# Second FFN of a fused attention and two-FFN kernel: each tile's last product moved one tile later, tile 1 turned by TensorE, other order of copies and joins

## Chip, cores, metric

The kernel runs on one core of a Trainium2 chip. The metric is the device time of one execution in microseconds (us); smaller is better. Engines are named as in the profile: PE (TensorE matmul), PEld (TensorE weight load), DVE (VectorE), ACT (ScalarE), POOL (GpSimd), SP (the queue that issues the DMAs).

## What is computed

Block attention over q, k, v of shape (2, 8, 768, 64), a first FFN with 2048 hidden columns, and a second FFN with 1024 hidden columns, all over 1536 tokens of width 512. The change touches the second FFN alone:

```python
def _moe2_ref(x, w_in, w_out, g_ln):          # x: 1536 x 512
    h = x @ w_in                              # 1536 x 1024
    h_max = np.max(h, axis=-1, keepdims=True)
    e = np.exp(h - h_max)
    sm = e / (np.sum(e, axis=-1, keepdims=True) + 1e-09)
    solu = h * sm
    mu = np.mean(solu, axis=-1, keepdims=True)
    var = np.mean((solu - mu) ** 2, axis=-1, keepdims=True)
    ln = (solu - mu) / np.sqrt(var + 1e-06) * g_ln
    return (ln @ w_out).astype(np.float32)    # 1536 x 512
```

## The kernel before, in words

The order of the program is written out by hand; every engine works through its own instructions strictly in that order, and semaphores make it wait for others. Each float32 factor of a product is split into a high and a low part, and a product is three passes (high x high, high x low, low x high).

The 1536 tokens are 12 tiles of 128 rows (t = 0 to 11), taken two at a time as pairs (p = 0 to 5; tiles 2p and 2p+1). For the first product a pair's input is combined into sums and split: `sum_xo` (4 subtractions or additions on POOL, L862) and `split_xo` (four pieces 0 to 3; a high part, on POOL a cast at L886 or on ACT at L884, and a low part on POOL, L887). With them seven products of six matmuls each, `emit_m(p, ...)` (L899, 42 in all), give both tiles' h: first products 1, 6, 7 and 5, each in a PSUM bank of its own (0, 1, 2 and 3), then 2, 4 and 3 in banks 0, 1 and 2 again. Before these three can write, the first four must be read: `emit_p1` copies bank 0 on ACT (L907), `emit_u2` and `emit_u3` read banks 1 and 2 on DVE (L911, L918), `emit_t5` bank 3 (L921). `emit_block` adds and takes the row maxima in PSUM (DVE, L930 to L936). The even tile ends in banks 1 and 3, the odd one in banks 0 and 2.

Then a tile t goes through these steps:

- `emit_exp2(t)`: exp on ACT from PSUM into e (L946), two halves; `emit_mult2(t)`: h times e on DVE (L952), which frees the tile's two banks.
- `emit_stats(t)` and `emit_factors(t)`: mean and variance on DVE (L961 to L974), and at the end a power on POOL, `pow` (L975).
- `emit_scaled(t)`: DVE takes the result of pow (L979) and scales e (L980).
- e must be turned for the last product, its columns on the partitions. By DMA: `emit_planes(t)` separates the two 16-bit halves on ACT (L1023, two instructions) and SP issues two DMA transposes (L1026); `emit_join(t, halves)` puts them together again, for each half of the tile a gather on ACT (L1036), the high part on ACT (L1039) and the low part on POOL (L1040), into the tile's place `ls`. By TensorE: `turn(t, banks)` makes 8 transposes into two banks (L1007), the high part on ACT (L1008), the low part on DVE (L1009). Before, tiles 0, 10 and 11 are turned by TensorE and the others by DMA.
- `emit_o2(t, bank)`: the last product, 24 matmuls (L1063), and `emit_out(t)`: a copy of the bank on ACT (L1073) and the output DMA.

PSUM has eight banks of this kind: four serve the even pairs, four the odd ones (`pair_banks`). `emit_o2` writes into banks of the pair before the current one, after `emit_mult2` has freed them, and the pair after next can use them once `emit_out` has copied them. The turned tiles have four places (`ls_places`, t % 4). The buffers "s" (three of 128 x 512) are shared in turn by `sum_xo` and `emit_join`; "raw" (three) by planes and turned planes.

In the loop before (L1207), step p holds: products of pair p, the join of tile 2p-2, last products of tiles 2p-3 and 2p-2, exp and statistics of the pair, the join of tile 2p-1, planes of tile 2p, sums and splits of pair p+2. Step 1 differs: pair 1's products come ahead of the loop, and its planes and join of tile 1 stand in the loop's tail:

```python
            if p == 1:
                emit_out(0)
                emit_planes(1)
            ...
            if p < NPT - 1:
                emit_planes(f)
            if p == 1:
                emit_join(1)
```

## Time and profile before

| | us |
|---|---|
| median of 3 runs | 499.28 (499.1 to 502.49) |
| the profiled execution's own time | 499.53 |
| its span, first to last instruction | 497.6 |
| busy in the span: PE, PEld | 471.0, 387.5 |
| busy in the span: DVE, ACT, POOL | 314.8, 319.5, 219.5 |

The profiled execution lasted 1.93 us longer than its span. A span is read from the first to the last instruction of any engine; a row of the timeline gives its start, its length, engine, line, operation, the tiles it writes and reads, and in brackets how long the engine stood idle ahead of it and what ended that. Rows that follow each other closely on one engine and line are merged, with a count. Matmuls are pipelined, so the distance between starts tells more than their lengths. The granted clock is given as a share of the full 2.4 GHz.

### The profile page before, as it was taken

Reading aid. Unit: us, or ns where it says so; the run is one execution under the profiler, and the core shown is the slowest. Engines: PE = TensorE matmul, PEld = TensorE weight load, DVE = VectorE, ACT = ScalarE, POOL = GpSimd, SP = SyncE. Lnnn points to the kernel's source line nnn. Section 1 sums busy time; section 2 is a strip of 40 time slices with the busy share of each in tenths; the row PEclk is TensorE's granted clock in tenths of the full one; section 3 lists DMA queues with packets and bytes.
Section 4 is the critical chain, followed back from the end, with each engine's and each line's share of the span. In section 5 each row is a group of like instructions: output and inputs, shape, how many; then the busy total and the mean of one; then the engine's idle time right before and its main releaser. Section 6 shows DMA issues by size and latency. Waiting matters only on the chain.

```text
span 497.6 us, 8050 instructions
## 1 busy us (share of the span) xinstructions
PE 471.0 (95%) x2907; PEld 387.5 (78%) x2907; DVE 314.8 (63%) x752; ACT 319.5 (64%) x566; POOL 219.5 (44%) x220
## 2 busy tenths in 40 slices
PE   8999899999999999999999999999997099999997
PEld 4878777778888888888888888888886088888886
DVE  3978775664444554746566465747999386877840
ACT  2688788757576756656655565657724677878721
POOL 2688788424323222222327237352054678683310
PEclk9999999999999999999999999999999589999999
DMA  7899974001332232232222121202102214133111
GB/s 214 243 237 236 227 197 137 5 1 43 106 106 86 88 122 88 84 112 100 86 96 74 42 85 44 85 1 84 43 1 63 63 23 126 42 87 105 42 43 43
DMA packets 59047, 46.18 MB, mean 93 GB/s; under 512 B 40448, under 2 KB 51328, under 8 KB 59008
## 3 DMA queue, kind: packets, MB, share of 16 engines
q1 hardware_dynamic: 59008, 45.67, 31.8%
q8 instruction: 23, 0.38, 0.3%
q14 instruction: 16, 0.13, 0.1%
HBM read 36.61 MB, written 3.15 MB: 80 GB/s over the span
## 4 chain that ended last, share of the span: by engine, by line
PE 77%; DVE 8%; ACT 4%; DMA 3%; POOL 3%; issue 2%; SPq 2%; POOLq 0%; ACTq 0%
PE y L319 25%; PE h L277 25%; PE h L1063 12%; PE h L899 9%; PE sps L562 2%; DMA vt<-in_v_dram 2%; PE vsum L473 1%; DMA qt<-in_q_dram 1%; DVE e L952 1%; PE aps L599 1%; SPq L445 1%; DVE e L980 1%; POOL sm L577 1%; POOL w L187 1%; ACT at L604 1%
## 5 line engine op out<-in xcount | busy, mean ns | idle before, releaser
L277 PE MATMUL h<-xs,w 128*128 128x512 f32 x576 | 141.2, 391 | 0.0
L319 PE MATMUL y<-gs,w 128*128 128x512 f32 x576 | 138.2, 389 | 0.0
L319 PEld LDWEIGHTS y<-gs,w 128*128 128x128 f32 x576 | 108.0, 188 | 22.5
L277 PEld LDWEIGHTS h<-xs,w 128*128 128x128 f32 x576 | 107.2, 188 | 21.6
L187 POOL TENSOR_TENSOR w<-s,w 128x512 fp32r<-128x512 f32 x32 | 41.7, 1303 | 102.8 <-ACT w L186 95.3
L286 ACT ACTIVATE r<-h 128x512 int32<-128x512 f32 x48 | 28.6, 597 | 87.1 <-PE h L277 87.0
L291 DVE SCALAR_TENSOR_TENSOR r<-r,h 128x512 f32<-128x512 int32 x48 | 33.0, 687 | 71.0 <-ACT r L286 70.8
L899 PE MATMUL h<-w,xo 128*128 128x512 f32 x252 | 60.9, 400 | 14.4 <-ACT p L907 14.4
L899 PEld LDWEIGHTS h<-w,xo 128*128 128x128 f32 x252 | 48.8, 194 | 25.1 <-ACT p L907 14.8
L1063 PE MATMUL h<-w,ls 128*128 128x512 f32 (+1 forms) x312 | 66.9, 373 | 0.0
L169 DVE SCALAR_TENSOR_TENSOR s<-raw 128x512 int32<-128x512 int32 x48 | 37.6, 783 | 44.6 <-ACT raw L163 43.4
L1063 PEld LDWEIGHTS h<-w,ls 128*128 128x128 f32 x312 | 55.3, 188 | 10.3
L296 ACT ACTIVATE r<-r,half_pi 128x512 f32<-128x512 f32 x48 | 34.6, 721 | 5.4 <-DVE r L291 5.3
L301 DVE TENSOR_TENSOR h<-h,r 128x512 f32<-128x512 f32 x48 | 33.0, 688 | 4.9 <-ACT r L296 4.8
L307 DVE TENSOR_TENSOR gs<-h,gs 128x512 fp32r<-128x512 f32 x48 | 32.7, 680 | 5.3 <-ACT gs L306 5.3
L1040 POOL TENSOR_TENSOR ls<-s,ls 128x512 fp32r<-128x512 f32 x18 | 23.3, 1293 | 20.4 <-ACT ls L1039 20.4
L162 ACT ACTIVATE raw<-raw 128x512 f32<-128x512 f32 x48 | 31.9, 664 | 0.2 <-DMA raw<-in_moe_w_in_dram 0.2
L163 ACT ACTIVATE raw<-raw 128x512 int32<-128x512 uint32 x48 | 32.0, 666 | 0.0
L770 POOL TENSOR_TENSOR w<-s,w 128x512 fp32r<-128x512 f32 x14 | 17.9, 1293 | 30.8 <-ACT w L769 30.8
L306 ACT ACTIVATE gs<-h 128x512 fp32r<-128x512 f32 x48 | 28.2, 587 | 0.4 <-DVE h L301 0.4
L577 POOL TENSOR_TENSOR sm<-sm,mx 128x480 f32<-128x480 f32 x24 | 24.6, 1025 | 8.0 <-DVE mx L573 8.0
L592 POOL TENSOR_TENSOR sm<-sm,ss 128x480 f32<-128x480 f32 x24 | 26.2, 1094 | 0.3 <-ACT at L604 0.2
(103 smaller groups left out, 666.1 us busy)
## 6 DMA issues: line engine op xcount, KB each, us to landing
raw<-in_moe_w_in_dram SPq DMA_DIRECT2D x24, 512.0 KB, 3.6
raw<-in_moe_w_out_dram SPq DMA_DIRECT2D x24, 512.0 KB, 3.6
vt<-in_v_dram SPq DMA_DIRECT2D x16, 240.0 KB, 5.3
kt<-in_k_dram SPq DMA_DIRECT2D x8, 384.0 KB, 5.1
qt<-in_q_dram SPq DMA_DIRECT2D x8, 384.0 KB, 6.8
out_dram<-osb SPq DMA_DIRECT2D x11, 256.0 KB, 2.0
vt<-vm SPq DMA_DIRECT2D x16, 72.0 KB
vt<-in_v_dram SPq DMA_DIRECT2D x16, 48.0 KB, 6.8
```

Source lines behind the costliest of these rows:

```text
L162: nc.scalar.activation(out=hw, in_=hw, func=AF.Prelu, scale=REBIAS, alpha=NEGATIVE)
L163: nc.scalar.activation(out=lw, in_=lw.bitcast(U32), func=AF.Copy, scale=TOP3)
L169: nc.vector.scalar_tensor_tensor(out=self.f32[i], in0=t[:, :, 1], scalar=3, in1=t[:, :, 0], op0=ALU.logical_shift_left, op1=ALU.bitwise_or)
L187: nc.gpsimd.tensor_tensor(out=w[:, 1, :], in0=f, in1=as32(w[:, 0, :]), op=ALU.subtract)
L277: nc.tensor.matmul(h, lhsT=w[:, a, f * P:(f + 1) * P], rhs=xs_of[tb, c][:, b_, :], start=(m == 0), stop=(m == 3 * KC - 1))
L291: nc.vector.scalar_tensor_tensor(out=r, in0=r.bitcast(I32), scalar=TWO_PI, in1=h_of[step], op0=ALU.mult, op1=ALU.subtract)
L296: nc.scalar.activation(out=r, in_=r, func=AF.Sin, scale=-1.0, bias=half_pi)
L301: nc.vector.tensor_tensor(out=h, in0=h, in1=r, op=ALU.mult)
L307: nc.vector.tensor_tensor(out=gs[:, 1, :], in0=r, in1=as32(gs[:, 0, :]), op=ALU.subtract)
L319: nc.tensor.matmul(y[e], lhsT=w[:, a, e * P:(e + 1) * P], rhs=gs[:, b_, :], start=(f == 0 and i == 0), stop=(f == GF - 1 and i == 2))
L899: nc.tensor.matmul(banks_of[p][BANK[m]], lhsT=x[:, a, s0:s0 + P], rhs=w2_of[m, c][:, b_, :], start=c == j == 0, stop=c == 1 and j == 2)
L1063: nc.tensor.matmul(o, lhsT=ls_of[t][f // 4][:, a, s0:s0 + P], rhs=w[:, b_, cols], start=(f == 0 and i == 0), stop=(f == NF2 - 1 and i == 2))
```

## The change

The loop over pairs begins at 3 in place of 1; steps 1 and 2 are written out ahead of it. Throughout, the last product of a tile comes one tile later than it did: in step p those of tiles 2p-4 and 2p-3 (before: 2p-3 and 2p-2), so that three tiles are left behind the loop in place of two. The even and odd tiles' results go to other banks (1 and 3 of the pair before, in place of 0 and 1). Tile 1 is turned by TensorE, not by DMA. `emit_join` can make the high part on POOL (L1042 after, a cast), and does so for tiles 5 to 9. The copy `emit_p1(2)` stands ahead of any planes; sums and splits of a pair stand elsewhere among the joins and pows. No product is left out or added but the 8 transposes of tile 1.

```diff
-        def emit_join(t, halves=(0, 1)):
+        def emit_join(t, halves=(0, 1), hi=nc.scalar):
...
-                nc.scalar.activation(out=l[:, 0, :], in_=as32(s), func=AF.Copy)
+                if hi is nc.scalar:
+                    nc.scalar.activation(out=l[:, 0, :], in_=as32(s), func=AF.Copy)
+                else:
+                    hi.tensor_copy(l[:, 0, :], as32(s))
...
-        for p in range(1, NPT):
...
+        def emit_xo(p):
+            sum_xo(p)
+            split_xo(p, (0, 1, 2, 3), nc.gpsimd)
+
+        def complete(p, *products):
+            for m in products:
+                emit_m(p, m)
+                emit_block(p, m)
...
+        O = banks_of[0]
+        emit_o2(0, O[3])
+        emit_exp2(2)
+        emit_exp2(3)
+        emit_mult2(2)
+        emit_stats(2)
+        sum_xo(3)
+        emit_factors(2)
+        emit_out(0)
+        banks_of[2] = pair_banks(2)
+        emit_m(2, 1, 6, 7, 5)
+        emit_p1(2)
+        emit_u2(2)
+        emit_mult2(3)
+        emit_u3(2)
+        turn(1, banks_of[1][1::2])
+        emit_scaled(2)
+        emit_planes(2)
+        split_xo(3, (0, 1), nc.gpsimd)
+        emit_stats(3)
+        emit_factors(3)
+        emit_t5(2)
+        emit_block(2, 5)
+        emit_scaled(3)
+        emit_planes(3)
+        split_xo(3, (2, 3), nc.gpsimd)
+        complete(2, 2, 4, 3)
+        emit_o2(1, banks_of[1][2])
+        sum_xo(4)
+        split_xo(4, (0, 1), nc.gpsimd)
...
+        emit_out(1)
+        banks_of[3] = pair_banks(3)
+        emit_m(3, 1, 6, 7, 5)
+        emit_p1(3)
+        emit_join(2, (0,))
+        split_xo(4, (2, 3), nc.gpsimd)
+        emit_exp2(4)
+        emit_exp2(5)
+        emit_join(2, (1,))
+        emit_u2(3)
+        emit_u3(3)
+        emit_mult2(4)
+        emit_t5(3)
+        emit_block(3, 5)
+        emit_stats(4)
+        emit_factors(4)
+        emit_mult2(5)
+        emit_scaled(4)
+        complete(3, 2, 4, 3)
+
+        for p in range(3, NPT):
             f, s = 2 * p, 2 * p + 1
             O = banks_of[p - 1]
...
+            hi = nc.gpsimd if p > 3 else nc.scalar
+            emit_o2(f - 4, O[1])
+            emit_join(f - 3, (0, 1), hi)
+            emit_o2(f - 3, O[3])
+            if p == 3:
+                emit_planes(4)
+                emit_xo(5)
             emit_exp2(f)
             emit_exp2(s)
+            emit_out(f - 4)
+            emit_stats(s - 2)
+            emit_factors(s - 2)
             emit_mult2(f)
...
+            emit_scaled(s - 2)
+            if p < NPT - 1:
+                emit_planes(s - 2)
+                emit_stats(f)
                 emit_out(f - 3)
...
+                banks_of[p + 1] = pair_banks(p + 1)
+                emit_m(p + 1, 1, 6, 7, 5)
+                emit_factors(f)
+                emit_p1(p + 1)
+                emit_join(f - 2, (0, 1), hi)
+                emit_mult2(s)
+                emit_u2(p + 1)
+                emit_scaled(f)
                 emit_planes(f)
...
+                emit_u3(p + 1)
+                emit_t5(p + 1)
+                emit_block(p + 1, 5)
+                complete(p + 1, 2, 4, 3)
...
+        emit_planes(s - 2)
+        emit_join(f - 2, (0, 1), nc.gpsimd)
+        emit_o2(f - 2, O[0])
...
+        emit_out(f - 3)
+        emit_mult2(s)
+        emit_scaled(f)
+        emit_join(s - 2, (0, 1), nc.gpsimd)
...
+        turn(f, O[1::2])
+        emit_out(f - 2)
+        emit_scaled(s)
+        emit_o2(s - 2, O[2])
+        turn(s, O[1::2])
...
```

ACT before, from the copy of tile 0's result (osb, L1073) to the copy p of pair 2 (L907); L1023 are planes of tiles 1, 2 and then 3, L1036 and L1039 the join of tile 1:

```order
L1073 ACTIVATE osb<-h_3825 128x512
L1023 ACTIVATE planes<-e 128x1024 x4
L1036 ACTIVATE s<-turned 128x2x512
L1039 ACTIVATE ls<-s 128x512
L1036 ACTIVATE s<-turned 128x2x512
L1039 ACTIVATE ls<-s 128x512
L1023 ACTIVATE planes<-e 128x1024 x2
L907 ACTIVATE p_4016<-h_3982 128x512
```

ACT after, at the same place; the two L1008 are the turned tile 1, L1023 the planes of tiles 2 and 3, the last row the copy p of pair 3:

```order
L1076 ACTIVATE osb<-h_3825 128x512
L907 ACTIVATE p_3967<-h_3939 128x512
L1008 ACTIVATE ls<-h_3759 128x512
L1008 ACTIVATE ls<-h_3761 128x512
L1023 ACTIVATE planes<-e 128x1024 x4
L1076 ACTIVATE osb<-h_3760 128x512
L907 ACTIVATE p_4121<-h_4093 128x512
```

The copy p of pair 2 moved from behind six planes and a join to right behind the copy of tile 0's result, and the copy of tile 1's result now stands behind the planes of tiles 2 and 3.

POOL before, from the second half of pair 4's split (L886, L887) on; the first L975 is the pow of tile 6, the second that of tile 7, between them the join of tile 5, and L862 begins the sums of pair 5:

```order
L886 CAST xo<-xsum 128x512
L887 TENSOR_TENSOR xo<-xsum,xo 128x512
L886 CAST xo<-X_75 128x256
L887 TENSOR_TENSOR xo<-X_75,xo 128x256
L975 TENSOR_TENSOR st<-st,mhalf 128x1
L1040 TENSOR_TENSOR ls<-s,ls 128x512 x2
L975 TENSOR_TENSOR st<-st,mhalf 128x1
L862 TENSOR_TENSOR xsum<-X_75 128x256
```

POOL after, from the pow of tile 4 (first row) over the join of tile 3 and the sums of pair 5:

```order
L975 TENSOR_TENSOR st<-st,mhalf 128x1
L1043 TENSOR_TENSOR ls<-s,ls 128x512 x2
L862 TENSOR_TENSOR xsum<-X_75 128x256
L862 TENSOR_TENSOR xsum<-xsum,X_75 128x256
L862 TENSOR_TENSOR xsum<-X_75,xsum 128x256
L862 TENSOR_TENSOR xsum<-X_75 128x256
```

and, behind the first half of pair 5's split, its second half, the pows of tiles 5 and 6 and the join of tile 4:

```order
L886 CAST xo<-xsum 128x512
L887 TENSOR_TENSOR xo<-xsum,xo 128x512
L886 CAST xo<-X_75 128x256
L887 TENSOR_TENSOR xo<-X_75,xo 128x256
L975 TENSOR_TENSOR st<-st,mhalf 128x1 x2
L1043 TENSOR_TENSOR ls<-s,ls 128x512 x2
```

The pow of a pair's second tile stood ahead of the next sums; now the pow of tile 5 stands behind the sums and the whole split of pair 5.

ACT after, in step 3, from the exp of tile 7 (L946) over the copies of tiles 2 and 3 (L1076) with the planes of tile 5 between them, to the copy p of pair 4:

```order
L946 ACTIVATE e,st<-h_4093,st 128x512
L946 ACTIVATE e,st<-h_4095,st 128x512
L1076 ACTIVATE osb<-h_3940 128x512
L1023 ACTIVATE planes<-e 128x1024 x2
L1076 ACTIVATE osb<-h_3942 128x512
L907 ACTIVATE p_4345<-h_4310 128x512
```

The planes of the odd tile now stand between the two copies of results; before, planes of the even tile stood there.

## Rows read from the trace of the kernel before

**Rows 1.** Cores: the core's span and its mean granted clock.

```profile
core 0: 497.6 us, clock 0.983
```

**Rows 2.** Waits of PE, 376 to 498: line, line waited for, total, times, longest.

```profile
PE h L899 <- ACT p L907: 14.4, 1, 14.4
```

**Rows 3.** Timeline of PE, 376 to 498: start us, length us, line, operation, tiles, count.

```profile
377.34 5.60 PE L899 MATMUL h<-w,xo 128*128 128x512 f32 x24
397.35 6.59 PE L899 MATMUL h<-w,xo 128*128 128x512 f32 x18 [14.41 <-ACT p L907]
403.78 11.04 PE L1063 MATMUL h<-w,ls 128*128 128x512 f32 x48
414.66 9.68 PE L899 MATMUL h<-w,xo 128*128 128x512 f32 x42
...
475.87 1.03 PE L1007 MATMUL h<-ident,e 128*128 128x128 f32 x8
476.66 5.72 PE L1063 MATMUL h<-w,ls 128*128 128x512 f32 x24
```

**Rows 4.** Windows: length, busy PE, PEld, DVE, ACT, POOL, then granted clock, DMA, GB/s.

```profile
386.00:388.00 2.00, 0.00 (x0) 0.00 (x0) 1.00 (x6) 2.00 (x3) 0.00 (x0) 0.50 0.37 86
...
402.00:404.00 2.00, 2.00 (x9) 1.61 (x9) 1.32 (x5) 0.00 (x0) 1.92 (x3) 0.97 0.00 0
```

**Rows 5.** Timeline, 345 to 397, of ACT around the hole.

```profile
379.28 0.59 ACT L1073 ACTIVATE osb<-h 128x512 f32<-128x512 f32 x1
...
387.00 1.32 ACT L1036 ACTIVATE s<-turned 128x1024 uint16<-128x1024 uint16 x1
388.35 0.63 ACT L1039 ACTIVATE ls<-s 128x512 fp32r<-128x512 f32 x1
...
394.81 2.00 ACT L1023 ACTIVATE planes<-e 128x1024 uint16<-128x1024 uint16 x2 [3.92 <-DVE e L980]
...
396.72 0.58 ACT L907 ACTIVATE p<-h 128x512 f32<-128x512 f32 x1
```

**Rows 6.** Tile turned: time of its DMA transposes from issue to landing.

```profile
DMA to landing us min/median/max: 2.7/2.8/2.8
```

**Rows 7.** Timeline, 345 to 397, of DVE ahead of the hole.

```profile
368.30 0.68 DVE L918 TENSOR_TENSOR rest<-h,u 128x512 f32<-128x512 f32 x1
...
371.09 1.27 DVE L1009 TENSOR_TENSOR ls<-h,ls 128x512 fp32r<-128x512 f32 x2
...
379.32 1.27 DVE L952 TENSOR_TENSOR e<-h,e 128x512 f32<-128x512 f32 x2
...
380.59 1.27 DVE L961 BATCH_NORM_STATS2 bn<-e 128x6 f32<-128x512 f32 x2
...
382.66 0.15 DVE L974 TENSOR_SCALAR st<-st 128x1 f32<-128x1 f32 x1
```

**Rows 8.** Timelines, L979 and L980 of DVE: beside a busy POOL, beside an idle one.

```profile
415.20 1.32 DVE L980 TENSOR_SCALAR e<-e,mv,st 128x1024 f32<-128x1024 f32 x1
...
455.42 0.16 DVE L979 TENSOR_TENSOR st<-st 128x1 f32<-128x1 f32 x1 [0.66 <-POOL st L975]
455.62 0.81 DVE L980 TENSOR_SCALAR e<-e,mv,st 128x1024 f32<-128x1024 f32 x1
```

**Rows 9.** Timeline of POOL, 414 to 428, a packed stretch.

```profile
413.90 0.55 POOL L975 TENSOR_TENSOR st<-st,mhalf 128x1 f32<-128x1 f32 x1 [0.58 <-DVE st L974]
414.42 0.73 POOL L862 TENSOR_TENSOR xsum<-X 128x256 f32<-128x256 f32 x1
...
417.76 0.60 POOL L886 CAST xo<-X 128x512 fp32r<-128x512 f32 x1
...
421.63 1.30 POOL L1040 TENSOR_TENSOR ls<-s,ls 128x512 fp32r<-128x512 f32 x1
...
425.07 0.62 POOL L886 CAST xo<-xsum 128x512 fp32r<-128x512 f32 x1
...
427.50 0.74 POOL L887 TENSOR_TENSOR xo<-X,xo 128x256 fp32r<-128x256 f32 x1
```

More of the change, by code (lines that the diff above doesn't have):

```diff
@@ L1208, in fused_kernel @@
+        for p in range(3, NPT):
             f, s = 2 * p, 2 * p + 1
             O = banks_of[p - 1]
-            if p > 1:
-                banks_of[p] = pair_banks(p)
-                emit_m(p, 1, 6, 7, 5)
-                emit_planes(s - 2)
-                emit_p1(p)
-                emit_u2(p)
-                emit_join(f - 2)
-                if p + 1 < NPT:
-                    split_xo(p + 1, (2, 3), nc.gpsimd)
-                emit_u3(p)
-                emit_t5(p)
-                emit_block(p, 5)
-                for m in (2, 4, 3):
-                    emit_m(p, m)
-                    emit_block(p, m)
@@ L1225, in fused_kernel @@
-            outs = (0,) if p == 1 else (f - 3, f - 2)
-            for k, o in enumerate(outs):
-                emit_o2(o, O[3] if p == 1 else O[k])
+            hi = nc.gpsimd if p > 3 else nc.scalar
[5 more added lines that the diff above has]
+                emit_xo(5)
             emit_exp2(f)
             emit_exp2(s)
+            emit_out(f - 4)
+            emit_stats(s - 2)
@@ L1230, in fused_kernel @@
+            emit_factors(s - 2)
             emit_mult2(f)
-            emit_stats(f)
-            emit_factors(f)
-            emit_mult2(s)
-            emit_scaled(f)
-            if p == 1:
-                emit_out(0)
-                emit_planes(1)
-            else:
-                emit_join(s - 2, (0,))
-                emit_out(f - 3)
-                emit_join(s - 2, (1,))
-            if p < NPT - 1:
-                emit_planes(f)
-            if p == 1:
-                emit_join(1)
@@ L1246, in fused_kernel @@
-            emit_stats(s)
-            emit_factors(s)
-            emit_scaled(s)
-            if p + 2 < NPT:
-                sum_xo(p + 2)
-                split_xo(p + 2, (0, 1), nc.gpsimd)
-            if p > 1:
-                emit_out(f - 2)
-        turn(f, O[2:4])
-        emit_o2(f - 1, O[0])
-        emit_out(f - 1)
-        turn(s, O[2:4])
-        emit_o2(f, O[1])
+            emit_scaled(s - 2)
+            if p < NPT - 1:
+                emit_planes(s - 2)
+                emit_stats(f)
+                emit_out(f - 3)
+                banks_of[p + 1] = pair_banks(p + 1)
[6 more added lines that the diff above has]
+                emit_scaled(f)
+                emit_planes(f)
+                emit_u3(p + 1)
+                emit_t5(p + 1)
+                emit_block(p + 1, 5)
+                complete(p + 1, 2, 4, 3)
@@ L1259, in fused_kernel @@
+        emit_planes(s - 2)
+        emit_join(f - 2, (0, 1), nc.gpsimd)
+        emit_o2(f - 2, O[0])
+        emit_stats(f)
+        emit_factors(f)
+        emit_out(f - 3)
+        emit_mult2(s)
+        emit_scaled(f)
+        emit_join(s - 2, (0, 1), nc.gpsimd)
+        emit_stats(s)
+        emit_factors(s)
+        turn(f, O[1::2])
[3 more added lines that the diff above has]
+        turn(s, O[1::2])
+        emit_out(s - 2)
+        emit_o2(f, O[0])
         emit_out(f)
-        emit_last((O[0], banks_of[NPT - 1][0]))
+        emit_last((O[2], banks_of[NPT - 1][0]))
```

## The prediction

> **What bounds the kernel now.** I read the view of cores first: the span is 497.6 us and the mean granted clock 0.983 [rows 1]. So the clock was low somewhere, for a short while. The page says that PE is busy for 95% of the span. The next view is who waited for whom over the second FFN's tail, from 376 us on: it holds one wait of PE, 14.4 us on L907, the copy p1 [rows 2]. PE's own rows in order of time show where it lies: 24 products of pair 2 start at 377.34, the next 18 start at 397.35, and from there to 494 nothing is idle [rows 3]. Those 18 lasted until 403.78, that is 6.43 us, where 18 at the full rate take 18 x 0.2267 = 4.08 (48 products take 414.66 - 403.78 = 10.88). The table of two-microsecond windows explains the other 2.35 us: the granted clock is 0.50 in the window that begins at 386, and 0.97 again only in that of 402 to 404 [rows 4]. It had fallen within about three microseconds after PE's last product ended, near 382.9, and returned about 5 us after the restart at 397.35.
>
> Why p1 came late is read in ACT's rows [rows 5]. ACT copied out(0) at 379.28 and then stood in its queue: planes of tiles 1 and 2, two turned halves of tile 1 (L1036, the first at 387.00), planes of tile 3 (394.81), and only then p1 of pair 2 at 396.72, whose input had been ready since about 379. So the tail is bound by PE but for one hole of 14.41 + 2.35 = 16.76 us, made by the order of ACT's queue and by the chain behind it (ACT's joins, POOL's subtractions and its pow at L975, DVE's L979 and L980, the planes again).
>
> **What the change does at that hole.** p1(2) now stands right behind out(0), so it is copied at 379.9. PE's four first products of pair 2 end near 382.8, and PE goes on. Tile 1 is turned by PE: 8 transposes, 0.79 us from start to next start (475.87 to 476.66) [rows 3]. All else that TensorE does is the same, so this 0.79 is the whole of PE's added work. Tile 1's planes (2.0 us of ACT), its joins (2 x (1.32 + 0.63)) [rows 5] and its two DMA transposes leave; in their place ACT copies two turned banks. This saves nothing beyond the hole, since ACT is not what ends PE's other waits: there are none. The DMA transposes of later tiles land 2.8 us after issue [rows 6], and now a whole tile's work of ACT stands between the planes and the join that reads them; I cost them at nothing, and at up to 2.8 us a join were that work gone.
>
> Does PE wait anew? I follow the chain with durations of before. DVE had finished the statistics of tile 2 at 382.8 [rows 7]. Behind them now stand u2(2) 0.7, the two products of tile 3 1.28, L954 0.15, u3(2) 0.7, the two L1009 of turned tile 1 1.28, L979 and L980 of tile 2 1.0, statistics of tile 3 1.28 and 0.9: 7.3 us, so 390.1. L980 lasts 0.81 alone and 1.32 beside a running POOL instruction [rows 8]; with three such waits of 0.5, at L954, L979 and L980, it is 391.6. I take 390.5, since POOL itself stands idle for part of this. Until then PE has m(2) with the transposes to 387.65, o2(1) to 393.1 and pair 3 from there; ls(1) is complete at about 387.2 and u3(2) frees the bank near 386, so nothing is late. out(1) stands on ACT behind the planes of tile 3 and comes at 394.6 to 396.0; m(3;7) needs its bank at 395.8: up to 0.2 us, left out.
>
> **Where the new wait is.** POOL's pow of tile 3 starts at 390.5, and from there POOL has no hole until the pow of tile 5. In the kernel before, the same kinds of work in a packed stretch give the prices [rows 9]: four sums of a pair 3.34 (414.42 to 417.76), two casts with their subtractions 3.87 (417.76 to 421.63), the other two, the last of half size, 3.17 (425.07 to 428.24), a join's subtraction 1.3, a pow 0.55. In the new order: 3 pows 1.65, three second halves of a split 9.51 (pairs 3, 4, 5), two sums (4, 5) 6.68, two first halves (4, 5) 7.74, four joins (tiles 2 and 3) 5.2: together 30.8, so the pow of tile 5 ends at 421.3. Behind it come L979 and L980 on DVE 1.0 (455.42 to 456.43) [rows 8], planes of tile 5 on ACT 2.0 and out(3) 0.6 [rows 5]: 424.9. out(3) is queued on ACT behind those planes, and PE's m(4;5) writes the bank that out(3) reads. That is the new order's cost: in the old one pow(5) stood ahead of the sums and splits of the next pair, now all of pair 5's sums and splits stand ahead of it.
>
> When does PE want that bank? From 393.1: 42 products 9.52 to 402.6; o2(2) then meets the second half of ls(2), whose subtraction ends at 390.5 + 16.7 = 407.2 on POOL where PE wants it at 405.8 (12 + 2 products into o2(2)): 1.4 us. So o2(2) and o2(3) end at 402.6 + 10.88 + 1.4 = 414.9, and 18 products later, at 419.0, PE stands before m(4;5). It waits 424.9 - 419.0 = 5.9 us. This sum hardly depends on the small waits ahead of it: what delays PE there shortens this wait.
>
> At 5.9 us the clock should fall as in rows 4, where it had fallen within three. What it costs is bounded by nothing (it stays up, or returns at once) and the 2.35 of the only such row; I take 2.35, as the wait is twice as long as the time in which it fell there. By the rows alone the clock may also stay up in a wait so much shorter than 14.4 us, which gives 491.1 (rival 1). The Trainium skill (TensorE: Matmul & The Clock Gate, section The HAM clock gate) has a rule that speaks against this order: an idle array is put back to half its clock, 1.2 in place of 2.4 GHz, and has to work for some time before it is whole again, so a wait costs more than its length. By it the sum is 493.4, without it 491.1. The trace agrees in the one case that it has, with 0.50.
>
> From there on PE is fed. After out(3) the chain to out(5) is p1 0.6, join(4) 4.0, planes(6) 2.0, join(5) on ACT 2.7, its last cast and subtraction on POOL 1.9, pow 0.55, L979 and L980 1.0 to 1.8, planes(7) 2.0, out 0.6 [rows 5, 8, 9]: 15.4 to 16.2 us, and a pair takes PE 10.88 + 9.52 = 20.4. Ahead of o2(8) out(6), planes(9) and join(8) follow each other (0.6 + 2.0 + 1.4 + cast 0.65 + subtraction 1.3, with hand-overs 6.3) within the 5.9 us that o2(7) gives: 0.4 us of wait. The end, from the transposes of tile 10 to the last output, has the same products as before, 497.6 - 475.87 = 21.7 us [rows 1, 3].
>
> **Sum.** 497.6 - 16.76 (hole and its clock) + 0.79 (transposes) + 1.4 (o2(2)) + 5.9 (m(4;5)) + 2.35 (clock) + 0.4 (o2(8)) = 491.7. The profiled execution took 499.53, that is 1.93 outside its span, and lay 0.25 above the median of 499.28: 491.7 + 1.93 - 0.25 = **493.4 us**, 1.2% less than before. The bounds of the unknown costs: with POOL free of any hole from 378.85 on, the sum_xo, pow and first split of pair 3 would run (3.34 + 0.55 + 3.87) to 386.6 and pow(5) would end 3.9 earlier; without the clock's fall 2.35 less; with DVE at 391.6 and each hand-over late, 3 us more. Together 487 to 496.5.
>
> **Rivals.** (1) The clock does not fall, or returns sooner: 491.1. For it speaks that 5.9 us is less than half of 14.4; against it, that it fell within three. (2) PE does not wait at m(4;5) at all, because POOL is faster than its packed rows: then 497.6 - 16.76 + 0.79 + 0.4 = 482.0, as time 483.7. Against it: even without any hole POOL's queue ends pow(5) at 417.4, and out(3) would come at 421.0. (3) The hole only moves: pow(3) comes late, and with it POOL's 30.8 us. At 395 in place of 390.5 the new wait is 10.4 us and the time 497.9, no change by more than 1% (which is about what a measurement of this kernel can tell from none). For it: ACT's joins wait for buffers "s" that POOL still reads, so ACT and POOL can hold each other up. Against it: in the chain above each cast on ACT still ends 0.1 to 2 us before POOL comes to it. (4) Slower: the wait repeats in pairs 4 and 5, because the joins' copies now stand on POOL (10 casts of 0.61, in tiles 5 to 9) and DVE's L979 and L980 collide with them. It decides from the point where the chain from out(3) to out(5) exceeds the pair's 20.4 us; beyond that each us counts twice. Against it: a collision costs 0.5 us [rows 8], and more than eight would be needed in one chain before the first is paid for. At 28 us in place of 16 it would cost 28 - 22.75 in the first pair and 28 - 20.4 in the second, 12.9 in all: 506.3. The Trainium skill (SBUF — State Buffer, section Who interferes with whom) says that DVE and POOL hold their shared port as an exclusive lock for a whole instruction; the trace agrees, with 0.5 us a time.
>
> **Chances.** The forecast with its wait and clock 0.55 (range of its own 490.5 to 496.5); rival 1 0.17; rival 2 0.06; rival 3 0.15; rival 4 0.07. Faster by over 1% means under 494.3: most of rival 1 and 2, and seven tenths of the forecast, 0.61; slower 0.07; the rest, 0.32, within 1%. The range is 488.5 to 498.5; it leaves out rivals 2 and 4 and the longest waits of rival 3.
>
> **What the profile after would show.** p1(2) ahead of the planes, no hole at 383; a PE wait of about 6 us at L899 near 419, released by the copy of out(3), with POOL busy without a break from about 391 to 421 and DVE's L979 waiting for L975; a granted clock of 0.50 around 422 to 429. Were POOL idle in that stretch, or PE's wait released by L907 or by ls, the chain is wrong; were the wait over 10 us, pow(3) was late.

## The result, and the profile after

The changed kernel took 496.11 us (median of 6 runs, 491.97 to 496.87); the kernel before, run beside it, 500.4 us (6 runs, 498.36 to 503.35). The ratio is 0.990, with a 95% interval of 0.985 to 0.995: faster, by about the 1% that such a measurement can tell from nothing. 493.4 was forecast, within 488.5 to 498.5. Here and below a ratio leaves out executions more than 1.5% above the fastest of the same kernel (one of e6, one of e10, and one of the kernel before beside e12), while a median takes them all.

The profiled execution after took 496.03 us. The view of cores, to be read against [rows 1]:

```profile
core 0: 494.3 us, clock 0.993
```

The waits of PE, 376 to 498 (line, line waited for, total, times, longest), against [rows 2]:

```profile
PE h L899 <- ACT osb L1076: 5.4, 1, 5.4
PE h L1066 <- POOL ls L1043: 1.0, 2, 0.6
PE h L899 <- POOL xsum L862: 0.3, 1, 0.3
```

The wait of 14.4 us for p is gone, and one of 5.4 us for the copy of a result stands in its place. PE in order of time, against [rows 3] (start, length, line, tiles, count; in brackets the idle time ahead; each count is one of matmuls, six of which make one product of `emit_m`):

```profile
379.13 5.61 PE L899 MATMUL h<-w,xo 128*128 128x512 f32 x24
384.58 1.03 PE L1007 MATMUL h<-ident,e 128*128 128x128 f32 x8
385.37 4.34 PE L899 MATMUL h<-w,xo 128*128 128x512 f32 x18
389.55 5.60 PE L1066 MATMUL h<-w,ls 128*128 128x512 f32 x24
394.99 2.88 PE L899 MATMUL h<-w,xo 128*128 128x512 f32 x12
398.15 7.08 PE L899 MATMUL h<-w,xo 128*128 128x512 f32 x30 [0.28 <-POOL xsum L862]
405.07 3.33 PE L1066 MATMUL h<-w,ls 128*128 128x512 f32 x14
409.04 8.02 PE L1066 MATMUL h<-w,ls 128*128 128x512 f32 x34 [0.63 <-POOL ls L1043]
416.90 4.24 PE L899 MATMUL h<-w,xo 128*128 128x512 f32 x18
426.54 8.46 PE L899 MATMUL h<-w,xo 128*128 128x512 f32 x24 [5.40 <-ACT osb L1076]
434.84 11.04 PE L1066 MATMUL h<-w,ls 128*128 128x512 f32 x48
445.72 9.68 PE L899 MATMUL h<-w,xo 128*128 128x512 f32 x42
455.24 11.49 PE L1066 MATMUL h<-w,ls 128*128 128x512 f32 x50
467.12 5.29 PE L1066 MATMUL h<-w,ls 128*128 128x512 f32 x22 [0.39 <-POOL ls L1043]
472.25 1.03 PE L1007 MATMUL h<-ident,e 128*128 128x128 f32 x8
```

No more than 0.8 us passes between pair 2's first four products and its next three: these are the transposes. What ends the new wait is read in the timelines of POOL, DVE and ACT, one chain (against [rows 5, 8, 9]); POOL works without a break between its first two rows here:

```profile
392.39 0.55 POOL L975 TENSOR_TENSOR st<-st,mhalf 128x1 f32<-128x1 f32 x1 [3.09 <-DVE st L974]
...
422.37 0.55 POOL L975 TENSOR_TENSOR st<-st,mhalf 128x1 f32<-128x1 f32 x1
...
422.95 0.16 DVE L979 TENSOR_TENSOR st<-st 128x1 f32<-128x1 f32 x1 [3.59 <-POOL st L975]
423.15 0.81 DVE L980 TENSOR_SCALAR e<-e,mv,st 128x1024 f32<-128x1024 f32 x1
...
424.00 2.00 ACT L1023 ACTIVATE planes<-e 128x1024 uint16<-128x1024 uint16 x2 [6.24 <-DVE e L980]
425.91 0.58 ACT L1076 ACTIVATE osb<-h 128x512 f32<-128x512 f32 x1
```

The pows are those of tiles 3 and 5; the planes are those of tile 5, and osb is out(3). The windows of two microseconds (busy PE, PEld, DVE, ACT, POOL, granted clock, DMA, GB/s), against [rows 4], show the clock at 0.50 from 426 on, in the two windows left out here too, and back in that of 432 to 434:

```profile
422.00:424.00 2.00, 0.00 (x0) 0.00 (x0) 1.01 (x3) 0.00 (x1) 0.92 (x2) 1.00 0.00 0
424.00:426.00 2.00, 0.00 (x0) 0.00 (x0) 1.86 (x7) 2.00 (x3) 0.00 (x0) 0.88 0.00 0
426.00:428.00 2.00, 1.46 (x4) 1.17 (x5) 2.00 (x6) 2.00 (x4) 0.55 (x1) 0.50 0.78 176
...
432.00:434.00 2.00, 2.00 (x10) 1.59 (x9) 1.10 (x3) 2.00 (x3) 0.16 (x1) 0.92 0.58 131
```

**Where the time went.** The span is 3.3 us shorter, but the changed part gained more. The start of pair 2's first product moved from 377.34 to 379.13, by 1.79 us, in code that the change does not touch: the first product of the first FFN already starts 1.7 us later. This is the row of that line in the kernel before (the two numbers joined by "to" are the first and the last start in us):

```profile
L277 PE MATMUL h<-xs,w x576: 388/389/501, 60.2 to 343.6; 128*128 128x512 f32 x192
```

and this in the kernel after:

```profile
L277 PE MATMUL h<-xs,w x576: 388/389/501, 61.9 to 345.4; 128*128 128x512 f32 x192
```

In the experiments below it starts anywhere from 58.7 to 65.7 us, so the part ahead of the change differs by 7 us among the profiled executions, of which each kernel has one. I therefore compare the **tail**: from the start of pair 2's first product to the end of the span. It was 497.6 - 377.34 = 120.3 and is 494.3 - 379.13 = 115.2: 5.1 us saved, where the sum of the prediction has 5.9.

### The profile page after: what moved, and what is told of

It reads as the page before. It is cut to its first block, busy times and chain, and to the rows that moved or that the text cites. A ratio compares the mean times of both kernels' runs of the same rounds, so it can differ in the third digit from the quotient of the medians.

```text
span 494.3 us, 8071 instructions
## 1 busy us (share of the span) xinstructions
PE 473.6 (96%) x2915; PEld 388.4 (79%) x2915; DVE 318.9 (65%) x754; ACT 307.4 (62%) x552; POOL 224.0 (45%) x228
## 4 chain that ended last, share of the span: by engine, by line
PE 63%; POOL 11%; DVE 11%; issue 6%; ACT 4%; SPq 3%; DMA 2%; POOLq 0%; ACTq 0%; DVEq 0%
PE y L319 25%; PE h L277 25%; PE h L1066 4%; PE h L899 4%; POOL xo L887 2%; POOL ls L1043 2%; SPq L445 2%; POOL xsum L862 1%; DVE bn L961 1%; PE sps L562 1%; POOL sm L577 1%; DVE sm L573 1%; POOL xo L886 1%; POOL w L187 1%; DMA vt<-in_v_dram 1%
## 5 line engine op out<-in xcount | busy, mean ns | idle before, releaser
L899 PE MATMUL h<-w,xo 128*128 128x512 f32 x252 | 61.9, 404 | 5.7 <-ACT osb L1076 5.4
L1023 ACT ACTIVATE planes<-e 128x1024 uint16<-128x1024 uint16 x16 | 16.0, 1049 | 18.4 <-DVE e L980 17.0
```

What stands on the lines that cost most here:

```text
L899: nc.tensor.matmul(banks_of[p][BANK[m]], lhsT=x[:, a, s0:s0 + P], rhs=w2_of[m, c][:, b_, :], start=c == j == 0, stop=c == 1 and j == 2)
```

## The experiments

Each kernel is the kernel before, the one after, or an earlier one of these, with the edit that is shown. "Tail" is as above. In the table, the ratio is to the kernel before, run beside it; its median there was 500.97 us for e1 to e4, 500.74 for e5 to e8, 500.18 for e9 to e11 and 498.82 for e12.

| kernel | tail, us | median, us | ratio, 95% interval |
|---|---|---|---|
| before | 120.3 | 500.4 | 1 |
| after | 115.2 | 496.11 | 0.990, 0.985 to 0.995 |
| e1 no sums and split of pair 5 | 107.7 | 485.78 | 0.973, 0.965 to 0.980 |
| e10 without two pieces | 109.2 | 491.17 | 0.979, 0.971 to 0.986 |
| e11 without one piece | 112.0 | 493.05 | 0.984, 0.978 to 0.990 |
| e2 5 us more on POOL | 119.5 | 501.33 | 1.001, 0.997 to 1.004 |
| e3 out(3) ahead of the planes | 112.8 | 492.27 | 0.983, 0.976 to 0.990 |
| e4 step 3 reordered | 110.8 | 490.12 | 0.979, 0.973 to 0.986 |
| e5 before, early reads | 117.3 | 496.09 | 0.992, 0.988 to 0.997 |
| e6 before, tile 1 turned by PE | 115.8 | 495.43 | 0.989, 0.985 to 0.993 |
| e7 after, high part on ACT | 113.4 | 493.16 | 0.988, 0.981 to 0.995 |
| e8 e4 with four orders more | 106.1 | 485.81 | 0.971, 0.966 to 0.977 |
| e9 e5 and e6 together | 114.6 | 493.49 | 0.987, 0.981 to 0.994 |
| e12 e9 with orders mended | 115.3 | 495.35 | 0.992, 0.988 to 0.996 |

### Is POOL's queue what PE waits for at pair 4? (e1, e2, e10, e11)

The theory is the one of the prediction: pow(5) stands behind pair 5's sums and split, and PE waits for what hangs on it. The four kernels change only the amount of POOL work ahead of pow(5).

e1, with the work taken away:

```diff
                 emit_planes(4)
-                emit_xo(5)
+                for i in range(4):
+                    xo_of[5, i] = xo_of[3, i]
```

> The changed kernel, but pair 5's products take the split input of pair 3, so POOL makes no sums and no splits for pair 5 (10.4 us of POOL work left out, and the results of tiles 10 and 11 with it); every other instruction stays. Measured from the start of pair 2's first product to the end of the span, the kernel before took 120.3 us and the changed one 115.2. Theory (PE waits at the fourth product of pair 4 because POOL's pow of tile 5 stands behind pair 5's sums and splits): that pow starts as soon as DVE has the statistics, near 418 in place of 422.4; the wait falls from 5.4 us to 1 to 2, and the clock falls little or not; 108.5 to 111.5. Rival (ACT's order alone, the copy of tile 3's result behind the planes of tile 5, sets the wait whatever POOL does): wait 5.4 us, 115.2.

e2, with work added:

```diff
                 emit_xo(5)
+                t5 = xo_of[5, 1]
+                for _ in range(4):
+                    nc.gpsimd.tensor_tensor(out=t5[:, 1, :], in0=z_of[5][0], in1=as32(t5[:, 0, :]), op=ALU.subtract)
```

> The changed kernel with four more subtractions on POOL (the low part of pair 5's second piece made again, same result), 1.25 us apart, between pair 5's split and the pow of tile 5. Theory: every us of POOL there is a us of PE's wait: the wait grows from 5.4 to 10.4 us and the stretch from pair 2's first product to the end from 115.2 to 120.2. Rival (POOL is not what ends last): no change, 115.2.

e10 (two pieces less) and e11 (`split_xo(5, (0, 1, 3), ...)` and one piece less):

```diff
-                emit_xo(5)
+                sum_xo(5)
+                split_xo(5, (0, 1), nc.gpsimd)
+                for i in (2, 3):
+                    xo_of[5, i] = xo_of[3, i]
```

> The kernel after the change, but of pair 5's split input the last two pieces (a cast and a subtraction each, 3.17 us of POOL) are taken from pair 3's, so that the results of tiles 10 and 11 are other ones; the rest stays. It shortens the wait of PE at pair 4's 5th first product from 5.4 to about 2.2 us, in one piece. Measure: the tail, 115.2 after the change, 107.7 with none of pair 5's sums and split. Theory (a wait of some 2 us brings the clock down as the two short waits in e4 did): tail 115.2 - 3.2 - 1.2 = 110.8 (110.2 to 112.0), granted clock near 0.5 in a window behind the wait. Rival (the clock stays up, as behind the 1.09 us in e1): 115.2 - 3.2 - 2.9 = 109.1 (108.4 to 109.8).

> As e10, but only the third piece of pair 5's split input (1.90 us of POOL) is taken from pair 3's; the results of tiles 10 and 11 are other ones. The wait of PE at pair 4's 5th first product should be about 5.4 - 1.9 = 3.5 us. Measure: the tail. Theory (the clock falls): 115.2 - 1.9 = 113.3, less up to 1.2 if it returns sooner, so 112.1 to 113.6. Rival (the clock stays up): 115.2 - 1.9 - 2.9 = 110.4.

Measured: PE's row at the place of the wait, in the timeline of e1,

```profile
419.03 5.74 PE L899 MATMUL h<-w,xo 128*128 128x512 f32 x24 [1.09 <-ACT osb L1076]
```

in that of e10,

```profile
425.81 5.76 PE L899 MATMUL h<-w,xo 128*128 128x512 f32 x24 [2.34 <-ACT osb L1076]
```

in that of e11,

```profile
424.88 7.33 PE L899 MATMUL h<-w,xo 128*128 128x512 f32 x24 [3.51 <-ACT osb L1076]
```

and in that of e2:

```profile
433.18 8.07 PE L899 MATMUL h<-w,xo 128*128 128x512 f32 x24 [10.62 <-ACT osb L1076]
```

Against the 5.40 us after the change, 3.17 us of POOL less shortens the wait by 3.06, 1.90 less by 1.89, and four subtractions more lengthen it by 5.22, where POOL's rows from pow(3) to the end of pow(5) became 5.24 us longer: one to one, so POOL's queue ahead of pow(5) is the cause. With all 10.4 us taken away 1.09 us is left, and then something else ends last: POOL stands idle for 5.53 us ahead of pow(5), which waits for DVE's statistics (L974). e1's tail came out 0.8 us below the range expected and far from the rival's 115.2; e2's is 119.5 where 120.2 was expected.

The same rows price the clock: 24 matmuls take 24 x 0.2267 = 5.44 us at the full rate [rows 3], and the row's length minus the overlap with the next shows what they took here. After e1's wait they took 5.58 (424.61 - 419.03), after e10's 5.60, after e11's 7.17. So e10's tail of 109.2 is that of the rival (the clock stays up), and e11's of 112.0 lies 0.1 below the range of its theory (the clock falls). In e10 the clock is 1.00 in each window from 422 to 434, also in the one behind the wait:

```profile
426.00:428.00 2.00, 2.00 (x9) 1.61 (x9) 1.96 (x5) 1.97 (x3) 0.01 (x1) 1.00 1.27 204
```

and the one behind the wait in e11, which begins 1.1 us after PE's restart:

```profile
426.00:428.00 2.00, 2.00 (x6) 1.56 (x5) 1.96 (x5) 1.97 (x3) 0.69 (x1) 0.50 1.07 171
```

### Can the wait be mended by order alone? (e3, e4, e8)

e3 takes the copy out(3) and p1(4) ahead of the planes of tile 5:

```diff
             emit_out(f - 4)
+            if p == 3:
+                emit_out(f - 3)
+                banks_of[p + 1] = pair_banks(p + 1)
+                emit_m(p + 1, 1, 6, 7, 5)
+                emit_p1(p + 1)
             emit_stats(s - 2)
...
```

> The changed kernel with the copy of tile 3's result and the copy p1 of pair 4 put ahead of the planes of tile 5 on ACT; POOL and DVE as they are. Theory: the wait at the fourth product goes, but DVE still stands in L979 until POOL's pow of tile 5 at 422.9, and u2 of pair 4 is behind it (0.16 + 0.81 + 1.28 + 0.95 + 1.28 + 0.15 + 0.69, ready near 428): PE waits at product 4 instead, from 423.7 to 428, 4.3 us; stretch from pair 2's first product to the end 111.5 to 114.2 with and without the fall of the clock. Rival (ACT's order alone is the cause): wait and clock loss go, 106.8.

Measured 112.8, as the theory has it. PE's wait is two products later (30 matmuls into pair 4 in place of 18), at the next thing that hangs on pow(5): u2(4), which stands on DVE behind L979:

```profile
426.64 4.63 PE L899 MATMUL h<-w,xo 128*128 128x512 f32 x12 [4.20 <-DVE u L911]
```

e4 reorders step 3 on POOL, ACT and DVE together; it is written out ahead of the loop:

```diff
-        for p in range(3, NPT):
...
+        sum_xo(5)
+        split_xo(5, (0,), nc.gpsimd)
...
+        emit_out(2)
+        emit_stats(5)
+        emit_factors(5)
+        emit_mult2(6)
+        emit_out(3)
+        banks_of[4] = pair_banks(4)
+        emit_m(4, 1, 6, 7, 5)
+        emit_p1(4)
+        emit_u2(4)
+        split_xo(5, (1, 2), nc.gpsimd)
+        emit_scaled(5)
+        emit_join(4)
...
+        split_xo(5, (3,), nc.gpsimd)
+        emit_planes(5)
...
+        for p in range(4, NPT):
...
-            if p == 3:
-                emit_planes(4)
-                emit_xo(5)
```

> The changed kernel with step 3 written in another order: of pair 5's POOL work only the sums and the first piece stand ahead of the pow of tile 5, two pieces between the pows of tiles 5 and 6, the last behind; the copy of tile 3's result, p1 of pair 4 and the join of tile 4 ahead of the planes of tile 5 on ACT; u2 and u3 of pair 4 further ahead on DVE. Theory: no wait of PE over 1.5 us is left between 395 and 460 and the clock stays up: 106.8 to 108.5 from pair 2's first product to the end, about 8 us less than the changed kernel. Rival (POOL's work only comes due elsewhere, at the join of tile 4): a wait of 3 to 5 us at the last product of tile 4, 110 to 113.

Measured 110.8: in the rival's range, but not for the rival's reason. The wait at pair 4's first products is gone, and tile 4's last product (the 24 matmuls from 427.90) runs without one; it is tile 5's last product that now waits for its join, and the clock falls there:

```profile
434.92 0.73 PE L1066 MATMUL h<-w,ls 128*128 128x512 f32 x2 [1.42 <-POOL ls L1042]
436.27 6.79 PE L1066 MATMUL h<-w,ls 128*128 128x512 f32 x22 [0.62 <-POOL ls L1043]
```

POOL itself stood idle for 5.49 us ahead of this join, waiting for ACT. On ACT the join of tile 5 stood behind the planes of tile 6, which waited 4.55 us for DVE's L980. The timeline of ACT in e4:

```profile
430.95 2.01 ACT L1023 ACTIVATE planes<-e 128x1024 uint16<-128x1024 uint16 x2 [4.55 <-DVE e L980]
432.86 2.53 ACT L1036 ACTIVATE s<-turned 128x1024 uint16<-128x1024 uint16 x2
```

e8 is e4 with four orders more:

```diff
-        emit_planes(3)
...
         emit_out(1)
+        emit_planes(3)
...
-        split_xo(4, (2, 3), nc.gpsimd)
+        split_xo(4, (2,), nc.gpsimd)
...
         emit_join(2, (1,))
+        split_xo(4, (3,), nc.gpsimd)
...
         emit_scaled(6)
-        emit_planes(6)
...
             emit_join(f - 3, (0, 1), hi)
+            if p == 4:
+                emit_planes(6)
             emit_o2(f - 3, O[3])
...
             emit_exp2(s)
+            if p == NPT - 1:
+                emit_join(f - 2, (0, 1), nc.gpsimd)
             emit_out(f - 4)
...
-        emit_join(f - 2, (0, 1), nc.gpsimd)
```

> The reordered step 3 (e4) with four more orders changed: the join of tile 5 ahead of the planes of tile 6 on ACT; the second half of tile 2's join ahead of the last piece of pair 4's split on POOL; the copy of tile 1's result ahead of the planes of tile 3 on ACT; the join of tile 8 ahead of the copy of tile 6's result and the planes of tile 9. Measure: the tail, 115.2 after the change, 110.8 in e4. Theory (each wait left in e4 came from one of these places in a queue): no wait of PE over 0.5 us from pair 2 on, the clock stays up, tail 104.6 to 106 (120.3 - 16.8 + 0.8 + 0.3 = 104.6), time about 484 to 487. Rival (a wait moves on, to the copies of results or to the joins of tiles 8 and 9, and takes the clock with it): 107 to 110.

Measured: a tail of 106.1, 0.1 above the theory's range, and 485.81 us, within it. All that the waits of PE from 376 us on hold is one row:

```profile
PE h L899 <- ACT osb L1076: 0.3, 1, 0.3
```

This is the best full version of the study: 2.9% less than before. Its interval (0.966 to 0.977) lies wholly below that of the change (0.985 to 0.995).

### What made the hole, and is the delay needed? (e5, e6, e9, e12)

e5 is the kernel before with pair 2's first products and their reads right behind out(0):

```diff
...
             if p == 1:
                 emit_out(0)
+                banks_of[2] = pair_banks(2)
+                emit_m(2, 1, 6, 7, 5)
+                emit_p1(2)
+                emit_u2(2)
+                emit_u3(2)
                 emit_planes(1)
```

> The kernel before with one thing moved: pair 2's four first products and their reads (p1, u2, u3) stand right behind the copy of tile 0's result, ahead of the planes of tiles 1 and 2; tile 1 is still turned by DMA, all later steps stay. Measure: the tail, from the start of pair 2's first product to the end of the span; 120.3 us in the kernel before, 115.2 after the change. Theory (the hole was made by the place of p1 in ACT's queue): no hole of 14 us at pair 2's second products; in its place short waits, 1.5 to 2 us ahead of tile 1's last product (for its join) and about 5 ahead of tile 2's (its join's subtractions stand on POOL behind pair 3's sums and split), with a clock loss of about 2.4: tail 111 to 115, about 112.8. Rival (ACT's joins and the chain behind them would end last anyway, wherever p1 stands): the hole goes on to the next product, tail 118 to 120.

Measured 117.3, between the two. The hole at p is gone, as the theory says, but it left more waits than I named: the waits of PE in e5 are

```profile
PE h L1063 <- ACT ls L1039: 3.5, 2, 3.2
PE h L1063 <- POOL ls L1040: 2.3, 2, 1.7
PE h L899 <- ACT osb L1073: 1.8, 1, 1.8
PE h L899 <- DVE u L911: 1.5, 1, 1.5
PE h L899 <- ACT p L907: 0.5, 1, 0.5
```

9.6 us in all, and the clock fell behind the wait at tile 2's last product (its 22 matmuls of tile 2 took 7.46 us where 4.99 is the full rate). So the place of p1 made the wait at that product, but moving it alone gives back only 3.0 of the 16.8 us: most of the time comes back at the things behind it, much as the rival has it.

e6 is the kernel before with only tile 1 turned by TensorE:

```diff
             if p > 1:
                 banks_of[p] = pair_banks(p)
                 emit_m(p, 1, 6, 7, 5)
+                if p == 2:
+                    turn(1, banks_of[1][1::2])
...
-                emit_planes(1)
...
-            if p == 1:
-                emit_join(1)
```

> The kernel before with only tile 1 turned by TensorE in place of DMA, its 8 transposes behind pair 2's four first products; p1 of pair 2 still stands behind the planes of tiles 2 and 3 on ACT. Measure: the tail, as above (120.3 before, 115.2 after the change). Theory (p1's place in ACT's queue makes the hole, the join of tile 1 only lengthens it): the hole is halved, as the planes of tile 3 no longer wait behind the join, about 7.9 us (383.6 to 391.5 on the clock of the kernel before), with a clock loss of 2.4 and 0.8 of transposes: tail about 114.6 (113 to 116). Rival (the DMA turn of tile 1 is the whole cause): no hole over 1 us, tail 104 to 107.

Measured 115.8, within the theory's range; the hole is the only wait of PE, 8.64 us where 7.9 was worked out:

```profile
393.55 6.83 PE L899 MATMUL h<-w,xo 128*128 128x512 f32 x18 [8.64 <-ACT p L907]
```

The clock took 2.6 us more (18 matmuls in 400.22 - 393.55 = 6.67 us where 4.08 is the full rate). This one part gives 4.5 of the 5.1 us that the whole change gives.

e9 joins the two, still without the later last product:

```diff
                 emit_u3(2)
-                emit_planes(1)
+                turn(1, banks_of[1][1::2])
...
-            if p == 1:
-                emit_join(1)
```

> The kernel before with the two moves of e5 and e6 together: pair 2's four first products and their reads ahead of any planes, and tile 1 turned by TensorE; the last product of a tile is not put one tile later, and all later steps stay. It asks whether the delay of the last product is needed at all. Measure: the tail, from the start of pair 2's first product to the end; 120.3 before, 115.2 after the change, 117.3 in e5, 115.8 in e6. Theory (without the delay, tile 2's last product comes at PE before its join, which stands on POOL behind pair 3's sums and first split): no hole at pair 2's second products beyond about 1 us, waits of 3 to 5 us in all at tile 2's last product, and a clock loss of 2 to 3 us: tail 110 to 114. Rival 1 (the waits of e5 stay as they were, since POOL's queue is the same): 115.5 to 117.5. Rival 2 (with tile 1's joins gone, the join of tile 2 is early enough and the delay is not needed): no wait over 1 us, 104 to 106.5.

Measured 114.6, above the theory's range by 0.6 and below rival 1's. The waits at tile 2's last product are 2.36 + 1.60 us, as the theory has them; what it had not is 2.69 us for out(2):

```profile
396.76 0.73 PE L1063 MATMUL h<-w,ls 128*128 128x512 f32 x2 [2.36 <-ACT ls L1039]
399.10 6.70 PE L1063 MATMUL h<-w,ls 128*128 128x512 f32 x22 [1.60 <-POOL ls L1040]
...
409.85 4.38 PE L899 MATMUL h<-w,xo 128*128 128x512 f32 x18 [2.69 <-ACT osb L1073]
```

Without the delay of the last product e9 is no slower than the whole change (114.6 against 115.2, and tails are known to about 1 us, see e7). That the delay itself gains anything is not shown.

e12 mends just these places: sums and first split of pair 3 ahead of pow(3), join(2) ahead of planes(3), out(1) and out(2) earlier:

```diff
+                if p == 2:
+                    emit_join(f - 2)
                 emit_planes(s - 2)
...
+            if p == 2:
+                emit_out(1)
             emit_exp2(f)
             emit_exp2(s)
+            if p == 2:
+                emit_out(2)
...
             emit_stats(f)
+            if p == 1:
+                sum_xo(3)
             emit_factors(f)
...
+            if p == 1:
+                split_xo(3, (0, 1), nc.gpsimd)
...
```

> e9 (the kernel before, pair 2's reads early, tile 1 turned by TensorE, no last product moved one tile later) with the places mended at which PE waited in it: sums and first split of pair 3 ahead of the pow of tile 3 on POOL, the join of tile 2 ahead of the planes of tile 3 on ACT, the copy of tile 1's result ahead of the exps of pair 2 and that of tile 2 right behind them. It asks whether the last product has to come one tile later at all. Measure: the tail, from the start of pair 2's first product to the end; 115.2 after the change, 114.6 in e9, 106.1 in e8. Theory (the orders decide, not the delay): no wait at tile 2's last product, about 2 us at pair 3's second first product for the copy of tile 2's result, which stands behind four exps: tail 104.5 to 108, about 106.5. Rival (without the delay a tile's turn and join are too long for PE's schedule, so that the waits only move): waits of over 4 us in all, with a fall of the clock, 109 to 113.

Measured 115.3, above both ranges. The waits it was built to remove are gone (1.6 us for u2 of pair 2 are left), and the old hole is back one pair later: p1(3) stands on ACT behind the planes of tile 5, as p1(2) had stood behind those of tile 3.

```profile
401.90 5.60 PE L899 MATMUL h<-w,xo 128*128 128x512 f32 x24
414.51 6.29 PE L899 MATMUL h<-w,xo 128*128 128x512 f32 x18 [7.01 <-ACT p L907]
```

In the kernel before, pair 3 had no such wait: counted from pair 2's first product, PE came there 14 us later. Whether an order exists that needs no later last product is left open; this one does not show it.

### The high part on POOL (e7)

```diff
-            hi = nc.gpsimd if p > 3 else nc.scalar
+            hi = nc.scalar
...
-        emit_join(f - 2, (0, 1), nc.gpsimd)
+        emit_join(f - 2, (0, 1), nc.scalar)
...
-        emit_join(s - 2, (0, 1), nc.gpsimd)
+        emit_join(s - 2, (0, 1), nc.scalar)
```

> The kernel after the change, with the high part of every join made on ACT, as before (the change makes it on POOL in tiles 5 to 9). Measure: the tail, 115.2 after the change. Theory (ACT has room there, and the casts on POOL end no wait of PE): no change, 114.7 to 115.7, and the wait at pair 4's 5th first product stays at 5 to 6 us. Rival (the move to POOL is needed, since ACT's queue ends the later chains): 1 to 3 us more, with waits of PE for ls or osb in pairs 4 and 5.

Measured 113.4, 1.3 below the theory's range. The wait at pair 4 is the same 5.41 us. Of the 1.8 us of difference 1.0 is the clock: behind this wait the 24 matmuls took 7.32 us (430.25 to 437.57), after the change 8.30. Another 0.5 lies in the end (21.5 in place of 22.05 us), 0.2 at tile 8. So the move to POOL shows no gain here, and two executions with the same wait differ by 1 us in what the clock costs: the tails are no better known than that.

## Why the prediction was right, step by step

In the table, "measured" is the distance between starts in PE's rows of after, less the number of matmuls x 0.2267 us (18 take 4.08, 24 take 5.44, 42 take 9.52, 48 take 10.88, 72 take 16.32). For the hole, 42 matmuls of pair 2 are measured in this way before and after.

| step | forecast, us | measured, us | from |
|---|---|---|---|
| hole and its clock | -16.76 | -16.81 | before 403.78 - 377.34 - 9.52 = 16.92; after 389.55 - 379.13 - 9.52 - 0.79 = 0.11 |
| transposes of tile 1 | +0.79 | +0.79 | 385.37 - 384.58 |
| pair 3's products | 0 (up to 0.2) | +0.56 | 405.07 - 394.99 - 9.52 |
| o2(2), o2(3) | +1.4 | +0.95 | 416.90 - 405.07 - 10.88 |
| wait at pair 4 | +5.9 | +5.56 | 426.54 - 416.90 - 4.08 |
| clock behind it | +2.35 | +2.86 | 434.84 - 426.54 - 5.44 |
| o2(8) | +0.4 | +0.69 | 472.25 - 455.24 - 16.32 |
| the end | 0 | +0.32 | 494.3 - 472.25 - 21.73 |
| sum | -5.9 | -5.1 | the tails differ by 5.1 |

**The hole.** Right, in place and cause. Its cause has two halves that each close part of it: e5 moves p1, e6 takes the join of tile 1 out of the chain. "This saves nothing beyond the hole" also held.

**The chain to pow(3).** With the 1.79 us by which all lies later, the forecast of 390.5 is 392.3; the row is 392.39. The value taken between the bounds of 390.1 and 391.6 was right to 0.1; of the three collisions on DVE that the upper bound allows for, one came (L954 took 0.85 us in place of 0.15). Rival 3 (pow(3) late) with its 497.9 is out.

**POOL's packed stretch.** 30.8 us were added up from single rows, and it lasted 422.92 - 392.39 = 30.5. The chain behind it (1.0, 2.0, 0.6) ends at 424.9 + 1.79 = 426.7 in the forecast and at 425.91 + 0.58 = 426.49 in the row. The four kernels with more or less work on POOL (e1, e2, e10, e11) show that this is the cause and not only an agreement of sums.

**The clock.** It fell, as forecast, and cost 2.86 us in place of 2.35: rival 1 (491.1) is out. The reason that was given, a wait twice as long as the time in which the clock had fallen in rows 4, did not hold, so there was some luck in this step: PE stopped near 421.1 (416.90 + 4.24) and the windows still show 1.00 from 422 to 424 and 0.88 from 424 to 426. From the 0.88 I estimate the fall at 425.5, over four microseconds after PE's stop and one before its restart. The rule of the Trainium skill that the prediction weighed (TensorE: Matmul & The Clock Gate, section The HAM clock gate), that an idle array is put back to half its clock, agrees with the row of 0.50 here.

**The small waits** were mis-sized: out(1) at pair 3's products was "left out" at up to 0.2 us and cost 0.56; o2(2) was 0.45 too dear, o2(8) 0.3 too cheap. Together with the other rows of the table they make the 0.8 us by which the gain fell short. Each of the three cost about 0.3 us more than the idle time in its brackets (0.28, 0.63, 0.39). The row at 398.15 names POOL's L862; that the wait is for out(1) is read in e8, where out(1) stands ahead of the planes of tile 3: pair 3's 42 matmuls, from 395.97 on, run without a wait there, though this same sum ends only at 398.97, after the 12th of them.

**Rival 2** (no wait) and **rival 4** (the wait repeats) are out: there is one such wait, and pair 5's 42 matmuls from 445.72 run without one. "A collision costs 0.5 us", on which rival 4 was weighed, is too small, though:

```profile
393.63 1.79 DVE L980 TENSOR_SCALAR e<-e,mv,st 128x1024 f32<-128x1024 f32 x1
...
409.52 1.24 DVE L979 TENSOR_TENSOR st<-st 128x1 f32<-128x1 f32 x1 [0.53 <-POOL st L975]
410.80 1.75 DVE L980 TENSOR_SCALAR e<-e,mv,st 128x1024 f32<-128x1024 f32 x1
```

Beside a packed POOL L980 took up to 0.98 us more than its 0.81 alone, and L979 1.08 more than its 0.16. The lock that the Trainium skill names (SBUF — State Buffer, section Who interferes with whom) agrees with that; the row in [rows 8] from which I took 0.5 was a mild case.

**From span to time.** The forecast span was 491.7 and the measured one is 494.3. Of the 2.6 us, 1.79 lie ahead of the change and 0.8 in the tail. The prediction took the part ahead of the change as fixed, from one execution. That is the step that was off the most. As a ratio 0.988 was forecast (493.4 / 499.28), and 0.990 was measured; the medians differ by 4.3 us, where 5.9 was forecast.

## What to carry to other kernels

When a change moves a hole out of a queue, list for each engine what now stands ahead of the next thing that the critical engine waits for, in each stage and not only in the first: here the hole of 16.8 us came back as 11.7 us of smaller costs, and orders alone then took 9 us of them away (e8). A price for a packed stretch added up from single rows was good to 1% (30.8 against 30.5 us), and the slope of a wait against added or removed work told a cause from a coincidence in four runs. Compare tails that begin at the change when the part ahead of it varies by more than the change is worth.

## What was not expected of the hardware

**Short waits and the clock.** Of the single waits, those of 1.09 (e1), 2.34 (e10) and 2.69 us (e9) left the clock at 1.00; behind those of 3.51, 4.20, 5.40, 7.01, 8.64, 10.62 and 14.41 us it cost 1.7, 1.8, 2.9 (1.9 in e7), 2.1, 2.6, 2.5 and 2.4 us, so from 5.40 us on the cost does not grow with the wait. But in e4 two waits of 1.42 and 0.62 us, with two matmuls between them, cost 1.64 us (22 matmuls in 442.90 - 436.27 = 6.63 us, not 4.99). The window of e4 in which PE restarts behind the second of them:

```profile
436.00:438.00 2.00, 1.73 (x4) 1.45 (x5) 1.96 (x3) 2.00 (x8) 1.92 (x3) 0.52 0.00 0
```

e9 has both in one execution. Behind its two waits of 2.36 and 1.60 us, again with two matmuls between them, the clock fell and cost 1.55 us (22 matmuls in 405.64 - 399.10 = 6.54 us); behind its single wait of 2.69 us it stayed up. The windows of e9:

```profile
400.00:402.00 2.00, 2.00 (x6) 1.52 (x6) 1.44 (x4) 2.00 (x7) 1.92 (x3) 0.50 0.00 0
...
410.00:412.00 2.00, 2.00 (x9) 1.65 (x10) 1.88 (x2) 0.00 (x0) 1.84 (x4) 1.00 0.94 210
```

So the longest single wait does not tell what the clock will cost. Why e4's 2.04 us brought it down and the 2.34 us of e10 and 2.69 us of e9 did not is not settled by these runs.

**The part ahead of the change.** The first product of the first FFN starts between 58.7 (e1) and 65.7 us (e7), in code that is the same in all of these kernels. In e1 PE waits ahead of it for 1.4 us in all for the loads of v (L473, tile vt), and its clock is 1.00 from 50 to 60 us; in e7 it waits for 7.2 us for these loads, and the clock is 0.76 in that stretch. The start lies at 63.0 us or later in five executions (e2, e4, e7, e8, e10), and in each of them the clock fell below 1.00 in the first 60 us. Why the loads come late in some executions is open.
